# A planner's order of work gets a string of leanings, and a layernorm step is moved

## The chip, the cores and the metric

One core of a Trainium2 chip runs the kernel. The metric is the time of one execution in microseconds (us), the median of several runs. The engines are TensorE (PE, matrix products; PEld is its weight loading), VectorE (DVE), ScalarE (ACT), GpSimd (POOL) and SyncE (SP, which here issues transfers). Each engine works through its own instructions in program order; semaphores tie the engines together.

## What is computed

A block of attention with a gate, on x of 2048 tokens by 1024, in fp32:

```python
xn = _layernorm(x)
s  = softmax(q k^T / sqrt(32)) v @ wo          # 32 heads of 32, q, k, v = xn @ wqkv
h  = xn @ w1 + b1                               # 1024 -> 3584
act = h * tanh(softplus(h))                     # mish
return x + s * silu(act @ w2)                   # 3584 -> 1024
```

## The kernel before, in words

Every large product is made of three fast ones: an fp32 operand is split into a high part and the rest ("low"), and high x high, high x low and low x high are added in PSUM (`THREE`, line 281). The scores and P·V have their own forms: a head's 32 rows of high and low parts are stacked to a contraction of 128, and P·V is four narrow matmuls side by side.

**Opening, v stage (lines 447 to 527).** The 16 tiles of 128 tokens are normalised and transposed, and the first half of v is made from them. For tile t: `ln_a` (VectorE statistics), `ln_r` (ScalarE logarithm and exponential of the variance), `ln_b` (four small VectorE steps), `ln_x` (ScalarE scales the tile), `ln_t` (TensorE transposes it, eight times 128x128), `ln_c` (ScalarE copies the high part out of PSUM, VectorE the low part, for two halves). `v_group(i, t, cut, between)` issues the 24 products of one tile and calls `between`, here the next tile's transposes, after `cut` of them. The loop at line 474 runs these as a pipeline: the products of tile t - 2, the copies of tile t - 1, the scaling of tile t. Later in this stage the second half of v is made.

**qk stage (lines 664 to 683).** q and k of four heads at a time, with the first score products of head 0 and their maxima between them. `later` is a heap of small steps that are due some ticks ahead; `later.flush()` at line 682 issues what is left, the last small transposition of head 0's maxima ("mtp", `turn`) among it.

**Scheduled stage (lines 694 to 1240).** All heads of the attention and the whole feed-forward part run together, in an order that `Plan` works out while the program is built. An `Op` has an engine, an expected duration (`MM` = 0.228 us a matmul), the Ops it needs, buffers that it takes and gives back ("rings": seven PSUM banks `b`, of which s, t and d may hold 2, 2 and 4), and perhaps a `key`, the time at which it is due. `Plan.run` (line 173) simulates the engines: for the engine that is free first, it takes among the Ops that are ready the one with the least key, `(not op.late, key)` at line 194, emits it, and adds its duration. What comes out is a fixed order of instructions on each engine; on the chip each one waits for its real semaphores. TensorE's candidates come from five streams:

- t (line 812): scores, transposed, followed by ScalarE's exponentials "p"; then GpSimd adds up the sums "z" (line 841), and P·V ("pv", line 859) follows in groups of 6, 5 and 5 key tiles (`GROUPS`, line 35), with the column sums "zp" behind the last
- s (line 730): scores of the next head, of which VectorE takes the maxima "mx" (line 736)
- h (line 993): xn @ w1, 24 products for one tile of 128 features and 512 tokens, followed by the twelve steps of mish on VectorE and ScalarE
- y (line 1083): act @ w2, added up by VectorE into yacc (line 1105)
- op (line 1182): the first part of the product with wo, when the rest runs out

At line 703 the plan is told when each PSUM bank comes free of the stage before it; its five engines all start at 0.

**End (lines 1244 to 1312).** The rest of the product with wo, times silu, plus x.

Of the kernel before, what the change touches and what calls it, by code (L numbers as in the profile page):

```python
# [45 lines left out]


class Later:

# [20 lines left out]
class Op:  # L70


    def __init__(self, eng, took, need=(), emit=None, take=(), give=(), key=None, col=False, late=0.0,
                 bytes_=0, then=None, first=False, both=False, urgent=0.0):
# [3 lines left out]
        self.end = None  # L78


class Plan:
# [62 lines left out]
    def do(self, op, when):  # L144
# [71 lines left out]
def body(ctx: ExitStack, tc: tile.TileContext, x, wqkv, wo, w1, b1, w2, out):  # L216
# [504 lines left out]
    def s_stream():  # L721
        for h in range(1, H):
# [3 lines left out]
            for qt in range(NT):  # L726
                for kc in range(4):
# [5 lines left out]
                    def mx(at, h=h, qt=qt, kc=kc, tiles=tiles):  # L733
                        if qt == 0 and kc == 0:
# [3 lines left out]
                    m = Op("PE", MM, key=slot * (16 * (h - 1) + qt + (kc + 1) / 4 - LEAD), need=[loaded[h]],  # L738
                           emit=mm, take=["s", "b"])
                    yield m  # L740
# [57 lines left out]
    def t_stream():  # L798
        pts = {}
        for T in range(NS):  # L800
# [4 lines left out]
            for c in range(4):  # L805
# [14 lines left out]
                m = Op("PE", MM, key=slot * (T + (c + 1) / 4), emit=mm, take=["t", "b"],  # L820
                       need=[m_there[h, c]] if (h, c) in m_there else [])
# [29 lines left out]
    def product(T, pts, size):  # L851
# [15 lines left out]
        if kt == NT - 1:  # L867

            need.append(adds[T])
        last_pv[h] = op("PE", PV * size, key=slot * (T + 1.5), need=need + [vt_[h]], emit=emit, col=True,  # L870
                        take=["o"] if kt == size - 1 else [], give=["v"] if kt == NT - 1 else [], then=then)
# [107 lines left out]
    def h_stream():  # L979
        for n in range(NC * FT):  # L980
# [7 lines left out]
            for k in range(KT):  # L988
                for a, b in THREE:
                    def mm(at, n=n, c=c, k=k, a=a, b=b, i=i, t=t):  # L990
                        if i == 0:
# [4 lines left out]
                    give = (["w1"] if last else []) + ([f"xc{k // HK}"] if f == FT - 1 and (i + 1) % (3 * HK) == 0 else [])  # L996
                    m = Op("PE", MM, key=tile_time * due, emit=mm,
                           need=([w1_ops[n]] if n else []) + ([xc_ops[c, k // 2 * 2]] if c else []),
# [9 lines left out]
    def mish(n, made, t):  # L1008
# [42 lines left out]

        o1 = op("DVE", 0.74, need=[made], emit=d1, take=["e"])
        p1 = op("ACT", 0.73, need=[o1], emit=a1)
        p2 = op("ACT", 0.69, need=[p1], emit=a2, take=["d", "b"], first=True)
        o2 = op("DVE", 0.75, need=[p1], emit=d2)
        p3 = op("ACT", 0.68, need=[p2], emit=a3, take=["r"])
        o3 = op("DVE", 0.69, need=[o2, p2], emit=d3, give=["e"])
        p4 = op("ACT", 0.73, need=[p3], emit=a4)
        o4 = op("DVE", 0.69, need=[p4], emit=d4)
        o5 = op("DVE", 0.69, need=[o4], emit=d5, give=[("d", p2), ("b", p2)])  # L1060
        o6 = op("DVE", 0.69, need=[o5, o3], emit=d6, give=["r"])
        p5 = op("ACT", 0.6, need=[o6], emit=a5, take=["act"])
        act_ops[n] = op("DVE", 0.69, need=[p5], emit=d7, give=[("d", t["own"]), ("b", t["own"]), "h"])

# [3 lines left out]
    def y_stream():  # L1068
        for m in range(W2S):
            w2_op(m, [m_there[0, 3]])  # L1070
        for B in range(NC * FT // YB):
            c, b = divmod(B, FT // YB)
            done = []
            for dh in range(2):
                for s in range(4):
                    t = {}
                    for j in range(YB):
                        n, m_ = YB * B + j, (B * 2 + dh) * YB + j
                        for i, (p, q) in enumerate(THREE):
# [11 lines left out]
                            m = Op("PE", MM, key=tile_time * due, emit=mm,  # L1091
                                   need=[act_ops[n], w2_ops[m_]], take=["d", "b"] if j == 0 and i == 0 else [], give=give,
# [248 lines left out]
```

## Time and profile before

| what | before |
|---|---|
| median of 3 runs | 3411.41 us (3411.32 to 3413.32) |
| the profiled execution | 3414.67 us |
| its span, first to last instruction | 3412.9 us |
| TensorE busy | 3389.4 us (99%) |
| VectorE, ScalarE, GpSimd busy | 2337.6, 1955.3, 2431.8 us |
| TensorE's mean granted clock | 0.999 |

A row of the timeline gives start, length, engine, line, what is written from what, and how many instructions are merged in it; in brackets stands the engine's idle time before it and what ended that. A row of a group gives the count, the busy time, the mean of one in ns, the idle time ahead of the group's instructions and what ended most of it. A row of a window gives its length, the busy time of PE, PEld, DVE, ACT and POOL with their counts, the granted clock, the share of the DMA engines and GB/s. Matmuls are pipelined: their rows overlap.

### The profile page before, as it was taken

The page shows a single profiled execution, that of the slowest core. Times are in us where ns is not written, and L with a number is a line of the kernel's source. Part 1 is how long each engine was busy: PE and PEld are TensorE (multiplying, and loading weights), DVE is VectorE, ACT ScalarE, POOL GpSimd, SP SyncE. Part 2 cuts the span into 40 slices and gives each one's busy share as a digit, 9 for nine tenths or more (in the row PEclk, how much of TensorE's full clock was granted, in tenths as well). Part 3 has the DMA queues.
Part 4 walks back from the last instruction along what each step waited for, and adds up shares of the span by engine and source line. Part 5 has one row for each costly group of instructions (what it writes and reads, how often), then busy time and mean ns, then how long its engine had stood idle before and what let it go on. Part 6 is the DMA issues. An engine that isn't in the chain of part 4 may idle for free.

```text
span 3412.9 us, 45611 instructions
## 1 busy us (share of the span) xinstructions
PE 3389.4 (99%) x17059; PEld 2493.5 (73%) x17059; DVE 2337.6 (68%) x3764; ACT 1955.3 (57%) x3112; POOL 2431.8 (71%) x724
## 2 busy tenths in 40 slices
PE   8999999999999999999999999999999999999999
PEld 7888887677777777777777677777777677777687
DVE  6111136877878777787878777877878788876533
ACT  5211113766667667666666676666666666666621
POOL 1333333988899998888888888888888888888700
PEclk9999999999999999999999999999999999999999
DMA  5977877433444454343334543343445443333482
GB/s 196 297 268 269 277 266 249 121 112 100 123 130 129 139 173 145 103 124 106 118 102 122 156 142 115 109 126 98 129 114 181 125 118 112 112 118 119 136 298 84
DMA packets 284321, 517.02 MB, mean 151 GB/s; under 512 B 88170, under 2 KB 134250, under 8 KB 261354
## 3 DMA queue, kind: packets, MB, share of 16 engines
q1 hardware_dynamic: 264244, 472.16, 45.1%
q10 hardware_dynamic: 19856, 41.95, 3.3%
q8 instruction: 135, 2.21, 0.3%
q14 instruction: 86, 0.70, 0.1%
HBM read 374.31 MB, written 138.67 MB: 150 GB/s over the span
## 4 chain that ended last, share of the span: by engine, by line
PE 97%; DVE 1%; DMA 1%; ACT 1%; issue 0%; SPq 0%; POOL 0%; ACTq 0%; DVEq 0%
PE y L1083 18%; PE h L993 18%; PE t L812 13%; PE s L730 13%; PE pv L859 13%; PE qk L656 10%; PE op L1182 5%; PE v L337 5%; PE zp L885 1%; DVE mx L736 1%; PE pt L400 0%; ACT p L268 0%; PE s L583 0%; DMA xr<-xs 0%; DMA w2r<-in_B_w_dram 0%
## 5 line engine op out<-in xcount | busy, mean ns | idle before, releaser
L841 POOL TENSOR_TENSOR z<-z,p 128x2048 f32<-128x2048 f32 x448 | 2066.8, 4614 | 170.5 <-ACT p L268 142.0
L268 ACT ACTIVATE p<-t,zero 128x512 f32<-128x512 f32 x2048 | 1384.4, 690 | 622.6 <-PE t L812 608.0
L736 DVE TENSOR_REDUCE mx<-s 128x1 f32<-128x512 f32 x1984 | 1329.3, 686 | 440.9 <-PE s L730 433.7
L1083 PE MATMUL y<-w,act 128*128 128x512 f32 x2688 | 935.5, 391 | 0.7 <-DVE yacc L1105 0.5
L812 PE MATMUL t<-qstack,kstack 128*128 128x512 f32 x2048 | 802.2, 393 | 0.7 <-ACT p L268 0.5
L730 PE MATMUL s<-kstack,qstack 128*128 128x512 f32 x1984 | 778.8, 394 | 1.4 <-DVE mx L736 1.1
L993 PE MATMUL h<-xr,w 128*128 128x512 f32 x2016 | 713.6, 391 | 2.1 <-ACT p L268 1.2
L1083 PEld LDWEIGHTS y<-w,act 128*128 128x128 f32 x2688 | 502.7, 188 | 120.7 <-issue 9.2
L812 PEld LDWEIGHTS t<-qstack,kstack 128*128 128x128 f32 x2048 | 384.3, 188 | 111.8 <-issue 19.5
L859 PE MATMUL pv<-p,v 128*32 128x512 f32 x4096 | 459.4, 594 | 0.0
L730 PEld LDWEIGHTS s<-kstack,qstack 128*128 128x128 f32 x1984 | 371.2, 188 | 119.1 <-issue 21.0
L993 PEld LDWEIGHTS h<-xr,w 128*128 128x128 f32 x2016 | 377.8, 188 | 85.5 <-issue 5.0
L656 PE MATMUL qk<-xc,qkw 128*128 128x512 f32 x1536 | 350.8, 389 | 0.0
L656 PEld LDWEIGHTS qk<-xc,qkw 128*128 128x128 f32 x1536 | 288.2, 188 | 59.9
L859 PEld LDWEIGHTS pv<-p,v 128*32 128x32 f32 x4096 | 123.3, 110 | 282.8 <-issue 282.1
L1105 DVE TENSOR_TENSOR yacc<-yacc,y 128x512 f32<-128x512 f32 x416 | 283.0, 681 | 51.9 <-PE y L1083 51.0
L841 POOL TENSOR_TENSOR z<-p,p 128x2048 f32<-128x2048 f32 x32 | 148.0, 4626 | 219.7 <-ACT p L268 144.7
L993 PE MATMUL h<-xc,w 128*128 128x512 f32 x672 | 241.8, 392 | 0.1
L279 DVE TENSOR_TENSOR qst<-qk,qst 128x512 fp32r<-128x512 f32 x64 | 44.3, 692 | 257.6 <-ACT qst L271 257.6
L271 ACT ACTIVATE qst<-qk 128x512 fp32r<-128x512 f32 x64 | 38.3, 598 | 307.1 <-PE qk L656 291.7
L644 POOL CAST pw<-praw 128x512 fp32r<-128x512 f32 x64 | 39.5, 618 | 232.4 <-DMA w1s<-pw 123.7
L337 PE MATMUL v<-vw,xc 128*128 128x512 f32 x768 | 181.3, 395 | 1.8 <-ACT xc L271 1.3
(94 smaller groups left out, 2370.8 us busy)
## 6 DMA issues: line engine op xcount, KB each, us to landing
w<-w1s SPq DMA_DIRECT2D x112, 1024.0 KB
w<-w2s SPq DMA_DIRECT2D x200, 512.0 KB
qstack<-qs SPq DMA_DIRECT2D x96, 256.0 KB
kstack<-ks SPq DMA_DIRECT2D x96, 256.0 KB
x<-in_A_x_dram SPq DMA_DIRECT2D x32, 512.0 KB
praw<-in_B_w_dram SPq DMA_DIRECT2D x64, 256.0 KB
qs<-qst ACTq DMA_DIRECT2D x32, 512.0 KB
w1s<-pw SPq DMA_DIRECT2D x32, 512.0 KB
```

What stands on the lines that cost most here:

```text
L268: nc.scalar.activation(out_, in_, fn, bias=zero if bias is None else bias, scale=scale)
L337: nc.tensor.matmul(ps, xc[t // 4][k // HK][:, a, k % HK, (t % 4) * P:(t % 4 + 1) * P], vw[i, k // 2][:, b, k % 2], start=n == 0, stop=n == ...
L656: nc.tensor.matmul(ps, w[:, a, k], xc[c][k // HK][:, b, k % HK], start=n == 0, stop=n == 3 * KT - 1)
L730: nc.tensor.matmul(sp_, qst[h % 3][:, qt * P:(qt + 1) * P], kst[h % 3][:, kc * 512:(kc + 1) * 512], start=True, stop=True)
L736: nc.vector.reduce_max(tiles["mx"][:, qt, kc:kc + 1], tiles[qt, kc], axis=AX.X)
L812: nc.tensor.matmul(tp, kst[h % 3][:, kt * P:(kt + 1) * P], qst[h % 3][:, c * 512:(c + 1) * 512], start=True, stop=True)
L841: nc.gpsimd.tensor_tensor(zs[h], pts[T - 1] if kt == 1 else zs[h], pts[T], ALU.add)
L859: nc.tensor.matmul(pv[h][c * DH:(c + 1) * DH, :], vt[h][:, k, :], pts[T - kt + k][:, c * 512:(c + 1) * 512], start=k == 0, stop=k == NT - 1)
L993: nc.tensor.matmul(t["h"], w1t[n][:, a, k], xts_[c][k // HK][:, b, k % HK], start=i == 0, stop=i == 3 * KT - 1)
L1083: nc.tensor.matmul(t["y"], acts[n][:, p, s * P:(s + 1) * P], w2t[m_][:, q], start=j == 0 and i == 0, stop=j == YB - 1 and i == 2)
L1105: nc.vector.tensor_tensor(ya, ya, t["y"], ALU.add)
L1182: nc.tensor.matmul(ps[t, dh], ohl[t // 4, k][:, a, s * P:(s + 1) * P], wt[k][:, b, r], start=k == 0 and i == 0, stop=k == KT - 1 and i == 2)
```

## The change

The choice among ready Ops gets a leaning in each 21 us of TensorE's planned time, one of nine, read from a string of 130 digits. Digit 0 changes nothing. Digit 1 makes the key of the mish steps 2 us smaller (earlier); 2 and 3 let a P·V group count as ready 2 or 4 us later while TensorE is in the wide shape; 4 makes the key of s 6 us larger (later); 5 that of t 4 us larger; 6 those of h and y 8 us smaller; 8 that of h 8 us larger. Digit 7 ("settled") puts TensorE's Ops that became ready less than 0.2 us ago behind all others of their class. Further, the plan starts with VectorE busy until 2.8 us. And in the opening tile 2's `ln_a`, `ln_r` and `ln_b` stand behind `ln_c(1)`, and tile 1's `v_group` has its cut at 18 products instead of 8.

```diff
+LEANINGS = ({}, {"mish": 2.0}, {"hold": 2.0}, {"hold": 4.0}, {"s": -6.0}, {"t": -4.0}, {"h": 8.0, "y": 8.0}, {"settled": 1.0},
+            {"h": -8.0})
+TURN = 21.0
+LEAN = ("83700575777567776073778780867478770777713777737708777777777777788"
+        "87070875777277747776787770073777876777775777777787567766771872000")
...
+    def lean(self):
+        n = int(self.at["PE"] / TURN)
+        return LEANINGS[int(LEAN[n])] if n < len(LEAN) else {}
...
+            lean = self.lean()
...
+                    if op.kind == "pv" and not self.col:
+                        r += lean.get("hold", 0.0)
...
-                    key = (not op.late, r - op.urgent if op.key is None else op.key)
+                    key = (not op.late, e == "PE" and now - r < 0.2 and "settled" in lean,
+                           (r - op.urgent if op.key is None else op.key) - lean.get(op.kind, 0.0))
...
     v_low(0, 7, nc.vector)
-    ln_a(2)
-    ln_r(2)
     xts[3] = x_load(3)
     for t in range(2, NT + 2):
-        if t < NT:
+        if 2 < t < NT:
             ln_b(t)
-        evac = v_group(0, t - 2, 21 if t == 2 else 8, (lambda: ln_t(t - 1)) if t <= NT else None)
+        evac = v_group(0, t - 2, {2: 21, 3: 18}.get(t, 8), (lambda: ln_t(t - 1)) if t <= NT else None)
         if t <= NT:
             ln_c(t - 1)
+        if t == 2:
+            ln_a(2)
+            ln_r(2)
+            ln_b(2)
         if t < NT:
             ln_x(t)
...
     plan.rings["b"] = [(t, i) for i, t in enumerate((0.0, 0.2, 0.3, 0.9, 1.5, 2.1, 2.7))]
+    plan.at["DVE"] = 2.8
```

The other lines of the diff give the Ops their kind: "s", "t", "h", "y", "pv" and "mish".

More of the change, by code (lines that the diff above doesn't have):

```diff
@@ L73, in __init__ @@
     def __init__(self, eng, took, need=(), emit=None, take=(), give=(), key=None, col=False, late=0.0,
-                 bytes_=0, then=None, first=False, both=False, urgent=0.0):
+                 bytes_=0, then=None, first=False, both=False, urgent=0.0, kind=None):
         self.eng, self.took, self.need, self.emit = eng, took, need, emit
@@ L77, in __init__ @@
         self.bytes, self.then, self.first, self.both, self.urgent = bytes_, then, first, both, urgent
-        self.end = None
+        self.kind, self.end = kind, None
 class Plan:
@@ L738, in s_stream @@
                     m = Op("PE", MM, key=slot * (16 * (h - 1) + qt + (kc + 1) / 4 - LEAD), need=[loaded[h]],
-                           emit=mm, take=["s", "b"])
+                           emit=mm, take=["s", "b"], kind="s")
                     yield m
@@ L818, in ex @@
                     act(pts[T][:, c * 512:(c + 1) * 512], tile_[0], AF.Exp, scale=SCALE)
-                m = Op("PE", MM, key=slot * (T + (c + 1) / 4), emit=mm, take=["t", "b"],
+                m = Op("PE", MM, key=slot * (T + (c + 1) / 4), emit=mm, take=["t", "b"], kind="t",
                        need=[m_there[h, c]] if (h, c) in m_there else [])
@@ L869, in product @@
             need.append(adds[T])
-        last_pv[h] = op("PE", PV * size, key=slot * (T + 1.5), need=need + [vt_[h]], emit=emit, col=True,
+        last_pv[h] = op("PE", PV * size, key=slot * (T + 1.5), need=need + [vt_[h]], emit=emit, col=True, kind="pv",
                         take=["o"] if kt == size - 1 else [], give=["v"] if kt == NT - 1 else [], then=then)
@@ L996, in h_stream @@
                     give = (["w1"] if last else []) + ([f"xc{k // HK}"] if f == FT - 1 and (i + 1) % (3 * HK) == 0 else [])
-                    m = Op("PE", MM, key=tile_time * due, emit=mm,
+                    m = Op("PE", MM, key=tile_time * due, emit=mm, kind="h",
                            need=([w1_ops[n]] if n else []) + ([xc_ops[c, k // 2 * 2]] if c else []),
@@ L1050, in d7 @@
                                            op0=ALU.mult, op1=ALU.subtract)
[L1052 to L1063, printed above, removed]
+        o1 = op("DVE", 0.74, need=[made], emit=d1, take=["e"], kind="mish")
+        p1 = op("ACT", 0.73, need=[o1], emit=a1, kind="mish")
+        p2 = op("ACT", 0.69, need=[p1], emit=a2, take=["d", "b"], first=True, kind="mish")
+        o2 = op("DVE", 0.75, need=[p1], emit=d2, kind="mish")
+        p3 = op("ACT", 0.68, need=[p2], emit=a3, take=["r"], kind="mish")
+        o3 = op("DVE", 0.69, need=[o2, p2], emit=d3, give=["e"], kind="mish")
+        p4 = op("ACT", 0.73, need=[p3], emit=a4, kind="mish")
+        o4 = op("DVE", 0.69, need=[p4], emit=d4, kind="mish")
+        o5 = op("DVE", 0.69, need=[o4], emit=d5, give=[("d", p2), ("b", p2)], kind="mish")
+        o6 = op("DVE", 0.69, need=[o5, o3], emit=d6, give=["r"], kind="mish")
+        p5 = op("ACT", 0.6, need=[o6], emit=a5, take=["act"], kind="mish")
+        act_ops[n] = op("DVE", 0.69, need=[p5], emit=d7, give=[("d", t["own"]), ("b", t["own"]), "h"], kind="mish")
     w2_took, w2_uses, w2_ends = {}, {}, {}
@@ L1090, in y_stream @@
                             due = YB * B + YB + Y0 + g * Y1 + (BEHIND if B >= NC * FT // YB - 2 else 0)
-                            m = Op("PE", MM, key=tile_time * due, emit=mm,
+                            m = Op("PE", MM, key=tile_time * due, emit=mm, kind="y",
                                    need=[act_ops[n], w2_ops[m_]], take=["d", "b"] if j == 0 and i == 0 else [], give=give,
```

## The prediction

> **What bounds the kernel now.** I read the page first, for the busy shares; then the groups of TensorE's instructions, for their counts and for the idle time ahead of them; then the timeline, for what one of each costs when nothing holds it up; then the granted clock in short windows.
>
> ```profile
> span 3412.9 us, 45611 instructions
> ## 1 busy us (share of the span) xinstructions
> PE 3389.4 (99%) x17059; PEld 2493.5 (73%) x17059; DVE 2337.6 (68%) x3764; ACT 1955.3 (57%) x3112; POOL 2431.8 (71%) x724
> ```
>
> ```profile
> L1083 PE MATMUL y<-w,act 128*128 128x512 f32 x2688 | 935.5, 391 | 0.7 <-DVE yacc L1105 0.5 <-ACT p L268 0.2
> L812 PE MATMUL t<-qstack,kstack 128*128 128x512 f32 x2048 | 802.2, 393 | 0.7 <-ACT p L268 0.5
> L730 PE MATMUL s<-kstack,qstack 128*128 128x512 f32 x1984 | 778.8, 394 | 1.4 <-DVE mx L736 1.1
> L993 PE MATMUL h<-xr,w 128*128 128x512 f32 x2016 | 713.6, 391 | 2.1 <-ACT p L268 1.2 <-DMA xr<-xs 0.8
> L859 PE MATMUL pv<-p,v 128*32 128x512 f32 x4096 | 459.4, 594 | 0.0
> ```
>
> ```profile
> L885 PE MATMUL zp<-z,ones 128*32 128x512 f32 x256 | 33.3, 592 | 0.4 <-POOL z L841 0.4
> L400 PE MATMUL pt<-ident_r,x 128*128 128x128 f32 x128 | 18.4, 291 | 9.0 <-ACT x L268 9.0
> ```
>
> ```profile
> L560 PE MATMUL mtp<-ident_r,hl 128*128 128x128 f32 x35 | 8.8, 250 | 2.9 <-DVE hl L279 2.9
> ```
>
> TensorE is the bound: 99% busy against 71% for the next engine. But its rows overlap (a row lasts 0.39 us and the next may begin sooner), so "busy" also hides short waits. What it loses is found by counting from start to start.
>
> ```profile
> 560.60 5.60 PE L656 MATMUL qk<-xc,qkw 128*128 128x512 f32 x24
> 566.04 1.07 PE L583 MATMUL s<-kstack,qstack 128*128 128x512 f32 x4
> ```
>
> ```profile
> 923.99 0.39 PE L993 MATMUL h<-xc,w 128*128 128x512 f32 x1
> 924.31 5.36 PE L859 MATMUL pv<-p,v 128*32 128x512 f32 x48
> 929.60 0.50 PE L812 MATMUL t<-qstack,kstack 128*128 128x512 f32 x1
> 929.94 0.40 PE L730 MATMUL s<-kstack,qstack 128*128 128x512 f32 x1
> ```
>
> ```profile
> 3408.46 0.69 DVE L1275 TENSOR_TENSOR y<-op,y 128x512 f32<-128x512 f32 x1 [3.95 <-PE op L1182]
> ```
>
> A full matmul costs (566.04 - 560.60) / 24 = 0.2267 us. One of the narrow pv records costs (929.60 - 924.31) / 48 = 0.110 us. Going into the narrow shape costs 924.31 - 923.99 - 0.227 = 0.09 more, coming out 929.94 - 929.60 - 0.227 = 0.11.
>
> Now the floor. Of 17059 records 4096 + 256 are narrow, 128 are transposes and 35 the small mtp; 12544 are full: 12544 x 0.2267 = 2843.7. Narrow: 4352 x 0.110 = 479.6. The shape changes 3 times per head (GROUPS, line 35, has three entries; zp rides behind the last), 96 x 0.20 = 19. Transposes 128 x 0.1 and mtp 35 x 0.1: 16. Sum 3358. The span leaves 3412.9 less about 8.4 (nearly all of the 9.0 ahead of the transposes lies before the first) less 4.4 behind the last matmul (3412.9 - 3408.46) = 3400. So TensorE loses **about 42 us in all**, and no order of its work gains more. I split this into three places: the opening, 8.4 to 35.4 (72 products and 32 transposes, 19.5 of 27.0, so 7.5 lost); the seam ahead of the scheduled stage, 2.9 of waiting and 1.7 of half clock, 4.6; and the rest, some 29, spread over that stage.
>
> **The opening (v stage).** These rows are TensorE, ScalarE and VectorE around the second and third token tile.
>
> ```profile
> 17.45 1.09 PE L400 MATMUL pt<-ident_r,x 128*128 128x128 f32 x8 [0.66 <-ACT x L268]
> 18.30 0.95 PE L337 MATMUL v<-vw,xc 128*128 128x512 f32 x3
> 20.55 0.73 PE L337 MATMUL v<-vw,xc 128*128 128x512 f32 x2 [1.31 <-ACT xc L271]
> 21.50 2.35 PE L337 MATMUL v<-vw,xc 128*128 128x512 f32 x6 [0.22 <-DVE xc L279]
> 23.65 1.91 PE L400 MATMUL pt<-ident_r,x 128*128 128x128 f32 x8
> 25.21 5.93 PE L337 MATMUL v<-vw,xc 128*128 128x512 f32 x24
> 30.98 1.04 PE L400 MATMUL pt<-ident_r,x 128*128 128x128 f32 x8
> ```
>
> ```profile
> 19.39 0.29 ACT L268 ACTIVATE rs<-var,zero 128x1 f32<-128x1 f32 x1 [2.00 <-DVE var L370]
> 19.72 0.29 ACT L268 ACTIVATE rs<-rs,zero 128x1 f32<-128x1 f32 x1
> 19.92 1.06 ACT L271 ACTIVATE xc<-pt 128x512 fp32r<-128x512 f32 x2
> 20.88 1.25 ACT L268 ACTIVATE x<-x,tmp,rs 128x1024 f32<-128x1024 f32 x1
> ```
>
> ```profile
> 17.64 1.28 DVE L368 BATCH_NORM_STATS2 st<-x 128x6 f32<-128x512 f32 x2
> ```
>
> ```profile
> 31.61 1.09 ACT L271 ACTIVATE xc<-pt 128x512 fp32r<-128x512 f32 x2 [1.66 <-PE pt L400]
> ```
>
> ```profile
> 32.24 1.29 DVE L279 TENSOR_TENSOR xc<-pt,xc 128x512 fp32r<-128x512 f32 x2 [2.72 <-ACT xc L271]
> ```
>
> Tile 1 is transposed at 17.45, but ScalarE copies it only at 19.92: it stands behind tile 2's logarithm, which waits until 19.39 for VectorE's statistics begun at 17.64. The diff puts statistics, logarithm and scale of tile 2 (ln_a, ln_r, ln_b; no DMA, so no queue moves) behind ln_c(1). In the steady rows the copies start 31.61 - 30.98 = 0.63 after the transposes and VectorE's lows 0.63 after that. So copies at 18.1, lows 18.7 to 20.0, and TensorE's first product of tile 1 moves from 20.55 to about 19.0, when the three at 18.30 are out.
>
> Tile 2 pays for it. Statistics from 20.0; the logarithm 19.39 - 17.64 = 1.75 later, 21.8; logarithm and exponential 0.62; the scaling starts 20.88 - 20.01 = 0.87 after them, 23.3, and ends 1.25 later, 24.55. Before, the transposes of tile 2 began at 23.65; the new cut of 18 puts 18 products ahead of them, 19.0 + 18 x 0.227 + 0.4 for tile 1's lows = 23.5. TensorE idles 1.1, transposes 24.6 to 25.5, and does the last six products until 26.8. VectorE has then done statistics of tiles 3 and 4 (1.75 each) and one scale, so tile 2's first low ends near 28.1, against two products available: TensorE idles 0.85 more. From 28.1 come 22 products and 8 transposes: the third group ends near 34.1. Before: 16 of the 24 at 25.21 are the second group, 8 the third; the transposes end at 31.8; 16 x 0.227 more is 35.4. **Gain 1.3.** Later tiles are TensorE-bound, so it is kept. ScalarE's evacuation of group 0 slips by 1.5 us, with eight banks to cover it.
>
> One thing can take it back: the clock.
>
> ```profile
> 15.40:18.80 3.40, 2.74 (x15) 2.12 (x16) 3.26 (x9) 0.81 (x1) 0.00 (x0) 1.00 0.57 182
> 18.80:22.20 3.40, 1.88 (x7) 0.91 (x7) 2.54 (x10) 2.70 (x5) 0.00 (x0) 1.00 0.01 2
> 22.20:25.60 3.40, 3.40 (x14) 2.90 (x13) 3.23 (x10) 1.61 (x5) 0.00 (x0) 0.50 0.00 0
> 571.80:575.10 3.30, 3.30 (x10) 2.54 (x10) 1.84 (x3) 1.57 (x4) 0.00 (x0) 0.50 0.91 214
> ```
>
> First number after the length is TensorE's busy time, third from the end its clock. 1.88 busy of 3.40 is followed by half clock for 3.4 us; 2.74 is not. My two idles fall in different windows and leave about 2.4 and 2.6 busy, nearer to 2.74, so I count full clock. At half clock 1.7 us are lost and the opening ends 0.4 behind: its range is -0.4 to +1.7.
>
> The Trainium skill, "TensorE: Matmul & The Clock Gate", section "Why this matters for your kernels", asks only for "No PE-idle gaps >~3µs between matmul bursts". By that rule neither idle could cost clock and the gain would stay 1.3. The trace disagrees with it: the longest idle before the drop at 22.2 was 1.31 us.
>
> **The seam.**
>
> ```profile
> 570.07 0.33 PE L560 MATMUL mtp<-ident_r,hl 128*128 128x128 f32 x1 [2.91 <-DVE hl L279]
> 570.39 0.70 PE L730 MATMUL s<-kstack,qstack 128*128 128x512 f32 x2
> ```
>
> ```profile
> 567.47 2.48 DVE L587 TENSOR_REDUCE mx<-s 128x1 f32<-128x512 f32 x4
> ```
>
> TensorE stands 2.91 us, and 571.8 to 575.1 goes at half clock (1.7 more). One would expect `plan.at["DVE"] = 2.8` to cure that, for VectorE's four maxima end at 567.47 + 2.48 = 2.8 after TensorE comes free. It doesn't: this mtp comes from `later.flush()` (line 682), ahead of anything the plan places. The plan's zero is then really 570.39, when VectorE is free. The plan will hold back the third s product, and the small turn of head 0, by about 2.8 us; TensorE fills in with h, of which one tile is 24 x 0.227 = 5.4 us. Cost 0, hidden by that tile; if the next weights are late, 1 at most; gain at most 1. VectorE loses some 2 us here and has 32% of idle time to recover.
>
> **The scheduled stage.** `kind=` and `lean()` issue nothing; they reorder the same instructions, so the floor stays. 78 of the 130 digits are 7 (among TensorE's candidates, one that became ready under 0.2 us ago stands back), 13 are 0. The rest shift h and y by 8 us of due time, t by 4, s by 6, a product pv by 2 or 4, the mish by 2.
>
> What can be had? The idle named in the group rows: 0.7 + 0.7 + 1.4 + 2.1 + 0.4 = 5.3, from some ten waits. Each hides another 0.39 - 0.23 = 0.16, together 6.9. The other 22 of the 29 is 2 ns on each of some 10000 matmuls: waits too short for a row, and matmuls that are simply slower, which no order cures. A product just released is exactly where the plan's clock and the chip's differ, and TensorE's queue is in order, so one that is late holds up all the others: digit 7 removes waits up to 0.2 us and shortens longer ones by one matmul. Against that, each new order makes its own misses. I take the 6.9 and 0.3 of the short ones: **7.2** (an estimate; bounds: +13, twice the named ones, and -9, priced below).
>
> Sum: 1.3 + 0 + 7.2 = 8.5 off the profiled execution's 3414.67, its span of 3412.9 and 1.8 around it. That execution is 3.3 above the median of the timed runs, so I take the same 8.5 off 3411.41: **3402.9**.
>
> **The rivals.**
>
> A. The stalls only move. The named waits have four different causes (exponentials, maxima, a DMA, an addition), each a miss of the plan by 0.2 to 1.2 us, more than 7 covers. Then only the opening gains: 3410.1. For it: some stalls lie where two causes meet. Against: most are single waits behind s and t, which 7 is made for.
>
> B. The forecast, but the opening drops to half clock: 3404.6.
>
> C. Slower. Standing back means that each t product in a stretch of 7 can start one matmul later, 0.227, and t has two banks, so ScalarE's exponential starts later too. Over the stage ScalarE has 43% idle and it costs nothing; but where a mish shares it with the exponentials it is the local bound (the 1.2 us ahead of h is a wait for an exponential), and what it loses there TensorE loses. It takes (6.8 + 1.3) / 0.227 = 36 of the 2048 t products to be slower by 0.2%; with 2%, 41 of them, 9.3 us are lost: 3419.4.
>
> D. The order removes twice the named waits, 13: 3411.4 - 1.3 - 13 = 3397.1.
>
> **Numbers.** Forecast 0.55 (own range 3399 to 3407), A 0.17, B 0.10, C 0.10, D 0.08. Range 3395 to 3412: it leaves out C and a little of D's low end. A measurement tells about 0.2%, 6.8 us, from no change: faster means under 3404.6. Four fifths of the forecast, D and half of B: 0.56. Slower, C and little less: 0.09. Within: 0.35.
>
> **What would show it.** Tile 1's copies near 18.1, first product near 19.0, two idles near 1 us before 29, clock 1.0 throughout: the opening is right. The mtp still waits 2.9 near 570: the seam is right. Idle ahead of y, t, s and h under 2 us together instead of 4.9, at the same counts: the stage is right. Idle with new releasers of the same sum is A; longer idle behind exponentials is C. Wrong altogether if the seam's wait vanishes, or if narrow groups no longer stand as 96.

## The result, and the profile after

The changed kernel takes **3401.21 us** (median of 6 runs, 3400.82 to 3401.47). The kernel before, run beside it, takes 3413.2 (6 runs, 3411.32 to 3415.51). The ratio is 0.9964, interval 0.9953 to 0.9975, so the change makes the kernel faster by 12.0 us, or by 8.5 to 16 us with the interval. The profiled execution takes 3401.16 us, with a span of 3399.4, against 3414.67 and 3412.9.

The page of the changed kernel, with the lines that answer to the first fence of the prediction:

```profile
span 3399.4 us, 45612 instructions
## 1 busy us (share of the span) xinstructions
PE 3379.6 (99%) x17059; PEld 2498.3 (73%) x17059; DVE 2352.3 (69%) x3764; ACT 1960.5 (58%) x3112; POOL 2431.8 (72%) x724
```

The counts are the same (one instruction more in 45612), and TensorE is still 99% busy. The page shows that the kernel has become shorter, but not where. The groups of TensorE's instructions show a first part of it (count | busy, mean ns | idle time ahead and what ended it):

```profile
L1102 PE MATMUL y<-w,act 128*128 128x512 f32 x2688 | 932.6, 390 | 0.2
L831 PE MATMUL t<-qstack,kstack 128*128 128x512 f32 x2048 | 798.7, 392 | 2.3 <-DMA qstack<-mt 1.4 <-DVE mx L755 1.0
L749 PE MATMUL s<-kstack,qstack 128*128 128x512 f32 x1984 | 775.7, 393 | 0.0
L1012 PE MATMUL h<-xr,w 128*128 128x512 f32 x2016 | 704.4, 390 | 0.0
L878 PE MATMUL pv<-p,v 128*32 128x512 f32 x4096 | 459.3, 594 | 0.0
```

The idle time of y, t, s and h has gone from 4.9 us to 2.5, and 1.4 of these 2.5 are a new wait of t for a DMA, qstack<-mt, which does not stand in the rows of before. That is a gain of 2.4 us in a kernel that gained 13.5 in this execution, so the rest lies in times that these rows do not count.

I therefore counted from start to start, as the prediction did for its floor, but for every pair of TensorE's records: the distance of two starts, less what the pair costs when nothing holds it up (0.227 us between wide products, 0.318 from a wide one into the narrow shape, 0.523 from the last narrow one out of it, and 0.114 more for the next). What is left over is lost time. This table gives it in us for three places, and for the scheduled stage by the size of the single loss. One profiled execution of each kernel stands behind its row.

| kernel | opening, to 40 us | seam, 555 to 580 us | stage, 580 to 3240 us | of it losses to 12 ns | 12 to 150 ns | over 150 ns (how many) |
|---|---|---|---|---|---|---|
| before | 7.7 | 5.4 | 23.8 | 9.3 | 6.3 | 8.2 (17) |
| after | 6.0 | 8.7 | 9.3 | 3.8 | 3.8 | 1.7 (3) |
| difference | -1.7 | +3.3 | -14.5 | -5.5 | -2.5 | -6.5 |

The **stage** gained twice what I forecast, more than half of it in losses that no row of the profile names. The **opening** gained about what I said, and the **seam** lost 3.3, where I had said nothing.

The waits of TensorE in the stage (waited for: us in total, times, longest), before:

```profile
PE h L993 <- ACT p L268: 1.2, 1, 1.2
PE s L730 <- DVE mx L736: 1.1, 3, 0.5
PE h L993 <- DMA xr<-xs: 0.8, 1, 0.8
PE t L812 <- ACT p L268: 0.5, 1, 0.5
PE y L1083 <- DVE yacc L1105: 0.5, 1, 0.5
PE zp L885 <- POOL z L841: 0.4, 1, 0.4
PE y L1083 <- ACT p L268: 0.2, 1, 0.2
```

and after, where one line is all that is left:

```profile
PE t L831 <- DVE mx L755: 1.0, 1, 1.0
```

The timeline of TensorE at the seam of the changed kernel (start, length):

```profile
568.38 0.47 PE L578 MATMUL mtp<-ident_r,hl 128*128 128x128 f32 x1 [2.91 <-DVE hl L295]
568.69 1.19 PE L749 MATMUL s<-kstack,qstack 128*128 128x512 f32 x2
569.68 1.05 PE L831 MATMUL t<-qstack,kstack 128*128 128x512 f32 x2
570.54 0.63 PE L1012 MATMUL h<-xc,w 128*128 128x512 f32 x1
572.54 0.77 PE L831 MATMUL t<-qstack,kstack 128*128 128x512 f32 x1 [1.38 <-DMA qstack<-mt]
573.11 3.62 PE L1012 MATMUL h<-xc,w 128*128 128x512 f32 x8
```

The wait of 2.91 us is unchanged, as forecast. New is the third t product, placed behind a single h product: it waits 1.38 us for the stored maxima of head 0, while eight h products stand behind it in TensorE's queue. That h could have run is seen in the experiment e7 below, where three h products go there at 569.78. The rows show a second cost: two s products take 1.19 us instead of 0.70 before. The window over this place has half clock throughout (third number from the end):

```profile
567.60:577.70 10.10, 7.95 (x19) 5.88 (x20) 2.86 (x8) 2.58 (x6) 0.00 (x0) 0.50 0.83 258
```

In the kernel before, the half clock at the seam lasted 3.41 us; here the clock record runs from 567.51 to 577.75, 10.24 us, three times as long.

### The profile page after: what moved, and what is told of

Its sections match the earlier page's. It is cut to its first block, busy times and chain, and to the rows that moved or that the text cites. A ratio compares the mean times of both kernels' runs of the same rounds, so it can differ in the third digit from the quotient of the medians.

```text
span 3399.4 us, 45612 instructions
## 1 busy us (share of the span) xinstructions
PE 3379.6 (99%) x17059; PEld 2498.3 (73%) x17059; DVE 2352.3 (69%) x3764; ACT 1960.5 (58%) x3112; POOL 2431.8 (72%) x724
## 4 chain that ended last, share of the span: by engine, by line
PE 99%; DVE 1%; ACT 0%; DMA 0%; issue 0%; SPq 0%
PE y L1102 18%; PE h L1012 18%; PE t L831 14%; PE s L749 13%; PE pv L878 13%; PE qk L674 10%; PE op L1201 5%; PE v L353 5%; PE zp L904 1%; PE pt L416 0%; PE s L601 0%; DVE mx L755 0%; DVE st L384 0%; PE mtp L578 0%; DMA x<-in_A_x_dram 0%
## 5 line engine op out<-in xcount | busy, mean ns | idle before, releaser
L1012 PE MATMUL h<-xr,w 128*128 128x512 f32 x2016 | 704.4, 390 | 0.0
L1012 PE MATMUL h<-xc,w 128*128 128x512 f32 x672 | 232.2, 394 | 0.0
```

The source lines that it names most:

```text
L1012: nc.tensor.matmul(t["h"], w1t[n][:, a, k], xts_[c][k // HK][:, b, k % HK], start=i == 0, stop=i == 3 * KT - 1)
```

## The experiments

After reading the two traces I held two theories of the stage. One: the gain is that of digit 7. A product just released stands back, and so the many short misses between the plan's clock and the chip's disappear, whatever the order is otherwise. The rival: the gain belongs to the one order that this string of digits reaches, and any other order has misses of its own. For the opening the question was whether the move gains anything by itself, for the seam what had placed the third t product so early. The times of all experiments, each beside the kernel before (the ratio is that of the runs, with its interval):

| kernel | median us (runs) | ratio | opening | seam | stage | to 12 / 12 to 150 / over 150 ns (how many) |
|---|---|---|---|---|---|---|
| e1_opening_alone | 3412.41 (10) | 0.9995 [0.9985, 1.0004] | 6.0 | 5.5 | 23.7 | 9.1 / 6.0 / 8.6 (14) |
| e2_dve_alone | 3413.94 (10) | 1.0001 [0.9992, 1.001] | 6.1 | 5.6 | 23.9 | 8.9 / 6.4 / 8.7 (20) |
| e3_all_settled | 3411.49 (10) | 0.9993 [0.9983, 1.0002] | 6.1 | 5.2 | 22.6 | 2.2 / 8.0 / 12.4 (32) |
| e4_no_dve | 3398.85 (4) | 0.9956 [0.9941, 0.997] | 6.1 | 5.8 | 9.9 | 3.9 / 3.8 / 2.3 (4) |
| e5_no_settled | 3412.76 (10) | 0.9989 [0.9978, 1.0] | 6.1 | 7.8 | 21.0 | 8.2 / 6.3 / 6.4 (15) |
| e6_rotated | 3413.19 (10) | 0.9991 [0.9979, 1.0002] | 6.1 | 8.9 | 22.1 | 4.5 / 6.6 / 11.0 (23) |
| e7_first_digit | 3411.29 (10) | 0.9987 [0.9975, 0.9999] | 6.1 | 5.8 | 22.0 | 4.0 / 7.1 / 10.9 (27) |
| e8_early_turn | 3396.94 (4) | 0.9938 [0.9913, 0.9962] | 6.1 | 3.7 | 9.1 | 3.8 / 3.6 / 1.7 (4) |
| e9_early_turn_banks | 3399.57 (5) | 0.996 [0.9946, 0.9974] | 6.1 | 6.0 | 9.5 | 3.9 / 3.9 / 1.7 (3) |
| e10_middle_digit | 3401.28 (5) | 0.9965 [0.9952, 0.9978] | 6.1 | 7.7 | 9.4 | 3.8 / 3.8 / 1.8 (3) |
| e11_banks_no_dve | 3398.13 (4) | 0.9956 [0.9941, 0.9971] | 6.1 | 4.7 | 9.9 | 3.9 / 3.8 / 2.3 (4) |
| e12_maxima_by_act | 3394.18 (5) | 0.9947 [0.9933, 0.996] | 6.1 | 1.6 | 9.4 | 3.9 / 3.5 / 2.0 (3) |

The interval belongs to the ratio of all runs, which is not that of the two medians: for e8 the medians alone give 0.9950. The kernel before had medians of 3413.64 (beside e1 to e4), 3413.98 (e5 to e8), 3413.8 (e9 to e11) and 3412.97 (e12).

### e1: the opening alone

The kernel before, with the move and the cut of the opening and nothing else.

```diff
-    ln_a(2)
-    ln_r(2)
     xts[3] = x_load(3)
     for t in range(2, NT + 2):
-        if t < NT:
+        if 2 < t < NT:
             ln_b(t)
-        evac = v_group(0, t - 2, 21 if t == 2 else 8, (lambda: ln_t(t - 1)) if t <= NT else None)
+        evac = v_group(0, t - 2, {2: 21, 3: 18}.get(t, 8), (lambda: ln_t(t - 1)) if t <= NT else None)
...
+        if t == 2:
+            ln_a(2)
+            ln_r(2)
+            ln_b(2)
```

> The kernel before with the moved tile-2 steps and the cut of 18 alone; plan as before. Theory: the opening is worth what both traces show at the seam's small turn (570.07 before, 568.38 after), 1.7 us, and everything behind is shifted whole: 1.7 us faster than before, seam and stage losing what they lost before (about 5.4 and 24 us of TensorE time). Rival: the shift changes the phase of the clock's windows or of the transfers, and the rest moves by more than 1 us either way.

The median is 1.2 us below that of the kernel before, but the interval of the ratio holds 1: no gain that can be told from none. In the profile the opening loses 6.0 instead of 7.7. What that 1.7 is, e2 showed.

### e2: VectorE's start alone

The kernel before with `plan.at["DVE"] = 2.8` alone; its opening is the old one.

```diff
     plan.rings["b"] = [(t, i) for i, t in enumerate((0.0, 0.2, 0.3, 0.9, 1.5, 2.1, 2.7))]
+    plan.at["DVE"] = 2.8
```

> The kernel before with VectorE's planned start at 2.8 us alone. The forecast said 0, at most 1 us either way, since the wait at the seam comes from later.flush(). Rival: this line is what lets a t product in front at the seam whose maxima are still on their way, and makes the seam lose 3.3 us more, as in the changed kernel; then this is some 3 us slower than before.

The time is that of the kernel before, and stage and seam lose what they lost before. But this run settles the opening, by accident. Its timeline of TensorE there, with the old order:

```profile
20.51 0.73 PE L337 MATMUL v<-vw,xc 128*128 128x512 f32 x2 [1.31 <-ACT xc L271]
21.46 1.67 PE L337 MATMUL v<-vw,xc 128*128 128x512 f32 x6 [0.22 <-DVE xc L279]
22.96 1.03 PE L400 MATMUL pt<-ident_r,x 128*128 128x128 f32 x8
23.75 5.72 PE L337 MATMUL v<-vw,xc 128*128 128x512 f32 x24
29.31 1.03 PE L400 MATMUL pt<-ident_r,x 128*128 128x128 f32 x8
30.10 5.71 PE L337 MATMUL v<-vw,xc 128*128 128x512 f32 x24
```

From 17.4 to 21.5 everything stands as in the kernel before, to 0.04 us and with the same idle times to 0.01, but the six products then take 1.67 us instead of 2.35. The two windows that had shown the drop before show none here:

```profile
18.80:22.20 3.40, 1.88 (x7) 0.95 (x6) 2.54 (x10) 2.70 (x5) 0.00 (x0) 1.00 0.01 2
22.20:25.60 3.40, 3.40 (x20) 2.87 (x20) 3.19 (x10) 1.91 (x5) 0.00 (x0) 1.00 0.00 0
```

And this is the same place in the changed kernel, with the move:

```profile
17.44 1.10 PE L416 MATMUL pt<-ident_r,x 128*128 128x128 f32 x8 [0.16 <-ACT x L284]
18.29 5.16 PE L353 MATMUL v<-vw,xc 128*128 128x512 f32 x21
24.50 1.09 PE L416 MATMUL pt<-ident_r,x 128*128 128x128 f32 x8 [1.05 <-ACT x L284]
25.34 2.09 PE L353 MATMUL v<-vw,xc 128*128 128x512 f32 x8
27.78 1.66 PE L353 MATMUL v<-vw,xc 128*128 128x512 f32 x6 [0.34 <-DVE xc L295]
29.28 1.04 PE L416 MATMUL pt<-ident_r,x 128*128 128x128 f32 x8
30.07 5.71 PE L353 MATMUL v<-vw,xc 128*128 128x512 f32 x24
```

The last row is the same work in both: 30.10 against 30.07, and the first product of e2 had started 0.05 us earlier (8.31 against 8.36). At equal clock the move is worth under 0.1 us. It only divides one idle stretch into two smaller ones (1.31 + 0.22 becomes 1.05 + 0.34). The 1.7 us are the half clock, which in the old order comes in one execution and not in the other.

### e3: digit 7 everywhere

```diff
-LEAN = ("83700575777567776073778780867478770777713777737708777777777777788"
-        "87070875777277747776787770073777876777775777777787567766771872000")
+LEAN = ("77777777777777777777777777777777777777777777777777777777777777777"
+        "77777777777777777777777777777777777777777777777777777777777777777")
```

> The changed kernel with the digit 7 in all 130 places. Theory: standing back from what was just released is what removes the stage's waits, in any string; the stage then loses some 12 us against 9.3 in the changed kernel and 23.8 before, and the time is within 3 us of the changed kernel. Rival: the other 52 digits, fitted place by place, make the gain; then the stage loses 18 or more and the time is 8 us or more above the changed kernel.

The first theory falls. The losses up to 12 ns go from 9.3 to 2.2, further down than in the changed kernel, so standing back does what it says. But the losses over 150 ns rise from 8.2 to 12.4, and nothing remains. The waits of TensorE in the stage are others than before, with four exponentials ahead of t among them:

```profile
PE h L1012 <- DMA xr<-xs: 1.3, 1, 1.3
PE y L1102 <- DVE yacc L1124: 1.3, 3, 0.5
PE t L831 <- ACT p L284: 0.9, 4, 0.3
PE s L749 <- DVE mx L755: 0.6, 2, 0.4
PE t L831 <- DVE mx L755: 0.5, 1, 0.5
```

### e4: without VectorE's start

```diff
-    plan.at["DVE"] = 2.8
```

> The changed kernel without VectorE's planned start at 2.8 us. If that line makes the longer seam, the seam loses 5.4 again instead of 8.7 and the kernel is up to 3 us faster, unless the digits were fitted to the plan with it. If the first digit (8, h stands back) makes it, the seam stays at 8.7.

2.4 us faster by the medians than the change (the ratios' intervals overlap), and the seam accounts for it: 5.8 instead of 8.7. Without the line the plan gives the third s product earlier (569.95, ahead of h), the third t product goes at 572.53 after a wait of only 0.25 us, and the half clock there lasts 3.4 us. The stage keeps its gain, although TensorE's order starts out quite different; more on this under e10.

### e5: the other digits without the 7

Each 7 of the string becomes 0, the rest stays.

```diff
-LEAN = ("83700575777567776073778780867478770777713777737708777777777777788"
-        "87070875777277747776787770073777876777775777777787567766771872000")
+LEAN = ("83000505000560006003008080860408000000013000030008000000000000088"
+        "80000805000200040006080000003000806000005000000080560066001802000")
```

> The changed kernel with every 7 replaced by 0: the 52 other digits stay. Theory (standing back makes the gain): the stage loses 18 to 24 us as before, time 9 us or more above the changed kernel. Rival (the fitted digits make it): the stage loses 9 to 14, time within 5 us of the changed kernel.

The short losses are back at 8.2, the long ones stand at 6.4, and the time is within 1.2 us of the kernel before. So neither the 7 alone (e3) nor the rest alone gives the stage's 14.5 us.

### e6: the same digits at other places

```diff
-LEAN = ("83700575777567776073778780867478770777713777737708777777777777788"
-        "87070875777277747776787770073777876777775777777787567766771872000")
+LEAN = ("88707087577727774777678777007377787677777577777778756776677187200"
+        "08370057577756777607377878086747877077771377773770877777777777778")
```

> The changed kernel with the string rotated by 64 places: the same digits in the same numbers, at other places (it begins with 8 as before). Theory (standing back): the time stays within 4 us of the changed kernel. Rival (fitted to the places): the stage loses 18 or more, 8 us above it.

The same kinds of digits in the same number, put elsewhere: short losses 4.5, long ones 11.0, and no gain. The profiled execution behind this row took 3416.41, 3.2 above its median. Of its 11.0, 4.0 lie in a half clock from 656.99 to 663.81, behind a wait of 2.9 us for stored maxima; without it 7.0 are left, close to the 8.2 of the kernel before. The short losses thus follow the number of sevens; the waits do not.

### e7: one digit, at the start

The first digit, which holds for the first 21 us, becomes 7 instead of 8.

```diff
-LEAN = ("83700575777567776073778780867478770777713777737708777777777777788"
+LEAN = ("73700575777567776073778780867478770777713777737708777777777777788"
```

> The changed kernel with its first digit 7 instead of 8, so that h doesn't stand back in the first 21 us. Theory for the seam: 8 puts t's third product ahead of h while the maxima it needs are still being stored, and TensorE waits with h products at hand; with 7 the 1.4 us wait for that transfer goes and half clock lasts 3.4 us and not 10.2: the seam loses about 5.4 and not 8.7, up to 3 us faster. Rival: VectorE's planned start makes it, and the seam stays.

One digit of 130 takes the stage from 9.3 us lost back to 22.0, so that this kernel is 10 us slower than the change and not up to 3 faster, as I had expected. The seam is better for it, 5.8 instead of 8.7: digit 8 makes the key of h larger, so in the changed kernel h stands back in exactly the stretch in which only h can run, and with VectorE's line that put the third t product so early. It takes both: the seam loses 8.7, 7.8, 8.9 and 7.7 in the four kernels with the digit 8 and the line (the changed kernel, e5, e6, e10), 5.8 with the digit alone (e4), and 5.2 to 5.8 with the line alone (e2, e3, e7). The waits of the stage in this kernel:

```profile
PE t L831 <- ACT p L284: 2.4, 7, 0.6
PE s L749 <- DVE mx L755: 1.1, 2, 0.7
PE y L1102 <- DVE yacc L1124: 0.3, 1, 0.3
PE y L1102 <- ACT act L287: 0.3, 1, 0.3
PE t L831 <- DVE mx L755: 0.3, 1, 0.3
```

The largest is t behind exponentials, the row that rival C expected. It is 2.4 us and not 9.3. That the 7 makes it isn't shown: in e3, where every digit is 7, the same row has 0.9, and in the kernel before 0.5.

### e10: one digit, in the middle

The 65th digit, which acts from about 1910 us of the trace, becomes 7 instead of 8.

```diff
-LEAN = ("83700575777567776073778780867478770777713777737708777777777777788"
+LEAN = ("83700575777567776073778780867478770777713777737708777777777777787"
```

> The changed kernel with one digit of 130 altered, the 65th (8 to 7), which acts from about 1910 us. Theory (the string is fitted to one exact order, and an order once left isn't found again): up to 1910 the stage loses what the changed kernel loses there, behind it the waits over 150 ns come back, 3 to 6 us in all. Rival (each digit has its worth in its own 21 us): under 1 us lost, all near 1910 to 1931.

It is told here because it belongs to e7. After e3 to e7 my theory was that the string is fitted exactly: change one decision, and the order is never found again. This falls too. Time and losses are those of the changed kernel, and so is the order: I compared the two orders of TensorE's products place by place, and the share of places with the same product (the same one of its stream, counted from the start) in each 200 us from 600 to 3200 is 1.00, except for 0.67 in 1800 to 2000 us. In e4 it is 0.08 at 600 to 800 us, and then 0.83 to 1.00. In e7 it stays between 0.07 and 0.75, and in e3, e5 and e6 between 0.04 and 0.72. So the gain is there where the order is reached, and some disturbances heal while others do not. The seam has the same order as well and yet loses 7.7 and not 8.7, with a half clock of 6.83 us and not 10.24: that part of the seam's 3.3 belongs to the execution. Why e4 returns to it and e7 doesn't stays open.

### e8: the turn of the third maxima earlier

The 2.91 us of the seam come from `m_tail`: the maxima of head 0's third group are copied and turned seven to ten steps after they are ready, which is at the very end. Here they go at steps 2, 4 and 5.

```diff
-        for t, fn in ((1, r1), (7, r2), (9, r3), (10, r4)):
+        for t, fn in ((1, r1), (2, r2), (4, r3), (5, r4)):
```

> The changed kernel with head 0's small steps due earlier (ticks 2, 4, 5 and not 7, 9, 10), so that the turn of its third group isn't left to the flush behind VectorE's last maxima. If that turn is the cause of the 2.9 us wait and of the half clock behind it, the seam's 8.7 falls to 1 or 2: 6 to 8 us faster. Rival: TensorE waits as long at the plan's first product that needs VectorE, and little is gained.

3396.94, 4.3 us below the change by the medians, less than the 6 to 8 expected. The wait is gone, the profiled execution has no half clock at the seam, and another wait is uncovered. From 600 us on TensorE's order is that of the changed kernel place by place, and so it is in e9 and e12, so that these three differ from it at the seam alone. TensorE there:

```profile
565.64 0.39 PE L749 MATMUL s<-kstack,qstack 128*128 128x512 f32 x1
568.70 0.50 PE L749 MATMUL s<-kstack,qstack 128*128 128x512 f32 x1 [2.67 <-DVE mx L605]
```

The second s product takes a PSUM bank out of which VectorE still takes the last four maxima. The wait is nearly as long as the one removed. That it brings no half clock seems to be luck of this execution: a window of the clock ends at 567.66, in the middle of it. Of the four timed runs two have a mean clock of 1.000 (3396.20, 3396.24) and two of 0.999 (3397.64, 3399.26).

### e9: free banks first

As e8, and the plan is given the banks in the order in which they really come free.

```diff
-    for i in (7, 6, 3, 1, 4, 2, 0, 5):
+    for i in (2, 6, 3, 7, 4, 5, 0, 1):
```

> The kernel with the early turn, and the scheduled stage's PSUM banks renamed so that its second product gets a bank that is free at once, and not one that VectorE's last maxima still hold. Theory: the 2.7 us that TensorE still stands at the seam go, and the seam loses under 1.5 us against 3.7 with the early turn and 8.7 in the changed kernel: 2 to 3 us faster than the early turn alone, about 3394. Rival: it then waits for the next bank or for the first exponentials, and gains under 1.

The wait for the bank goes, and the kernel is not faster than e8 but slower by 2.6 us of the medians (the ratios' intervals overlap). TensorE runs on to 573 and then stands longer than ever:

```profile
573.09 0.39 PE L749 MATMUL s<-kstack,qstack 128*128 128x512 f32 x1
577.02 1.19 PE L831 MATMUL t<-qstack,kstack 128*128 128x512 f32 x2 [3.54 <-DMA qstack<-mt]
```

SyncE's queue in the same stretch shows why: the small store of head 0's last maxima is issued only at 572.31, behind a load of weights whose issue holds the queue for 4.14 us.

```profile
568.08 4.14 SPq L291 DMA_DIRECT2D w<-w1s  x1
572.31 1.32 SPq L291 DMA_DIRECT2D qstack<-mt  x2
```

### e11: e9 without VectorE's start

```diff
-    plan.at["DVE"] = 2.8
```

> As the kernel with early turn and renamed banks, without VectorE's planned start at 2.8 us. With the turn gone the plan's zero is the time at which VectorE still has 2.8 us to do, so the line is right here: without it the plan puts s products and the next turn ahead of VectorE's real time, and the seam loses 1 to 3 us more. Rival (as in the changed kernel, where leaving it out gained 2.3): the same or faster.

This expectation failed. With the turn gone I took the line to be right about VectorE, and to be missed. Without it the median is 1.4 us lower, and the seam loses 4.7 instead of 6.0. The line does no measured good in any of the three pairs (before and e2, e4 and after, e11 and e9).

### e12: the store from another queue

As e9, and the store of head 0's last maxima is issued by ScalarE instead of SyncE.

```diff
         def r6(at):
             for a in range(2):
                 move(qst[h % 3][96 + a:97 + a, first * P:(first + n) * P]
-                     .rearrange("o (t p) -> o t p", p=P), tiles["mt"][n * a:n * a + n, :])
+                     .rearrange("o (t p) -> o t p", p=P), tiles["mt"][n * a:n * a + n, :],
+                     None if h else nc.scalar)
```

> As the kernel with early turn and renamed banks; only head 0's last maxima are stored from ScalarE's queue and not from SyncE's, where in that kernel they were issued at 572.3 behind a weight transfer whose issue lasted 4.1 us, though ScalarE had them ready at 570.3. Theory (the seam's last wait is SyncE's order): the t product that stood 3.5 us goes at about 574 and not 577, the half clock behind it goes too, and the kernel is 2 to 4 us faster than that one (3399.6), about 3396.5. Rival (the 16 DMA engines are full with the weights, whoever issues): the landing stays near 577 and the time within 1 us of 3399.6.

**3394.18 us**, the lowest median of all: 18.8 us below the kernel before (ratio 0.9947, 0.9933 to 0.996). ScalarE issues the store as soon as it has copied the maxima:

```profile
570.44 1.80 ACTq L291 DMA_DIRECT2D qstack<-mt  x2
```

and TensorE has no wait at this place any more:

```profile
573.15 0.39 PE L749 MATMUL s<-kstack,qstack 128*128 128x512 f32 x1
573.41 0.70 PE L832 MATMUL t<-qstack,kstack 128*128 128x512 f32 x2
```

The seam loses 1.6 us and the clock is 1.00 from 560 to 580. From e9 to e12 that is 4.4 us of lost time less: the wait of 3.54 and the half clock that it brought both go. (By the medians it is 5.4 us, or 4.6 if each is taken against its own runs of the kernel before; the intervals of the ratios overlap.)

The earlier issue is only a part of it. The issue begins 1.9 us earlier (570.44 against 572.31), but the store's eight packets of 512 bytes end 3.3 us earlier: they run from 571.77 to 572.97 in e12, and from 575.96 to 576.23 in e9, where they start 2.3 us after their issue has ended and among the packets of the weights (8192 bytes each, from 572.85 on) that share their queue. In e12 such packets begin at 573.20, when the store has landed. Whether the other queue or the earlier time put the store ahead of them, no run takes apart. The Trainium skill, "DMA: Bandwidth & Descriptors", section "Issuing engines are not separate DMA queues", says that the DMAs of all issuing engines run on the same 16 DMA engines. Its table of rules adds that spreading them over the engines "only saves sequencer issue time". Such a saving is seen here, the 1.9 us behind one load's issue of 4.14; by the packets it doesn't cover the whole 3.3.

Whether e12 beats e8 isn't settled, since the intervals of their ratios overlap.

## Why the prediction was right, and where it wasn't

The forecast was 3402.9, the result 3401.21, inside the forecast's own range. But the sum came out by two errors of opposite sign, and the reason that I gave for the stage didn't hold, so that the closeness of the number is luck.

**The bound.** TensorE as the bound, the floor, and counting from start to start held. Before, the three places lose 36.9 us by the finer count, where I had about 42; 3.8 of the difference is the unhindered distance, 0.227 here and 0.2267 there, on 12544 products. The 96 changes of shape are still 96, and the narrow pv records have the same mean of 594 ns.

**The opening (1.3 forecast, 1.7 in the profile).** The schedule I wrote down is what the trace shows: tile 1's copies at 18.14 against 18.1, its first product right behind the three at 18.29, an idle of 1.05 against 1.1, and a second of 0.34 against 0.85. But the comparison was wrong. I measured my new schedule against an execution that held a half clock, and took "1.88 busy of 3.40 is followed by half clock" as a rule. In e2 the same stretch with the same 1.88 is followed by full clock. At equal clock the move gains under 0.1 us, and the 1.7 comes only where an execution of the old order happens to drop. The failed step is that one on the clock. One of the two traces of the old order drops there, and none of the twelve with the move, so the move may spare some executions the drop; how many isn't measured. The timed gain of e1 (1.2 us, its interval holds 1) can't be told from nothing.

**The seam (0 forecast, 3.3 lost).** That the mtp still waits 2.91 was right, and so was that VectorE's start doesn't cure it. The step that failed is "TensorE fills in with h". The first digit is 8, which makes h stand back just there, and together with VectorE's line, which holds back the third s product, it put first a t product that the chip could not yet do. Either alone leaves the seam at 5.2 to 5.8 (e2, e3, e4, e7). I had listed what each digit does, and had not applied the first one to the first stretch. The wait costs 1.78 us from start to start, and the longer half clock the rest, of which the execution decides 1 us (e10).

**The stage (7.2 forecast, 14.5 gained).** For the named waits 6.9 were forecast and 6.5 measured (losses over 150 ns, from 8.2 to 1.7), but not by the step that I gave. That step, "digit 7 removes waits up to 0.2 us and shortens longer ones by one matmul", failed for the long waits: with 7 in every place (e3) the losses over 150 ns rise to 12.4, and from e3 to e7 and in e10 they stay low only where the order comes back to that of the changed kernel (e4, e10). I also wrote that most waits are single ones behind s and t; in the rows four of nine are theirs, 1.6 of 4.7 us, and the most time, 2.0, is that of h. Mis-sized was the term of the short losses, of which I wrote "waits too short for a row, and matmuls that are simply slower, which no order cures" and took 0.3. They gave 5.5 up to 12 ns and 2.5 from there to 150 ns, 8.0 together. That an order can take the short losses down is shown by e3 (9.3 to 2.2) and by e5, where they return with the sevens gone. How it does so is only argued. In the kernel before, counting losses to 12 ns alone, the ten products behind a loss of over 150 ns lose about 3.5 ns more each than the others (4.4 against 1.0), and a product that was released well before its turn may leave no such trail. No run takes this apart, nor says why this one order has so few long waits.

**The rivals.** A, that stalls only move, is what e3, e5, e6 and e7 show: four orders out of the same planner, all within 2.7 us of the kernel before by their medians. Their stages lose 21.0 to 22.6 against 23.8, in other places. I gave it 0.17, which was too little for a change of order as such; that this order does better is a property of this order. B did not occur in the changed kernel. C's row appears in e7 at 2.4 us, a quarter of my price. D's 13 us from the order did come in size (14.5), but not as twice the named waits: 8.0 of them are losses to 150 ns. The seam took a part of them back.

## What to carry to other kernels

Where an engine is 99% busy, count its time from start to start against the unhindered distance and add the losses up by place and by size: here it found 23.8 us in the stage where the rows of idle time named 5.3, and it kept apart three places that the total had mixed. Before a gain is credited to a change of order, disturb the order (rotate it, change its first step): here an order was worth 14 us in the stage by where it ended up, while the rule alone (e3) and the other digits alone (e5) brought no gain that the times can tell. And when a wait goes, look at once for the next thing in line (here a bank, then a queue), for the third removal gave what the second had not.

## What the runs showed of the hardware

**The half clock comes in whole windows, and their phase decides.** Behind the opening its lengths are 3.41 us (before, twice), 6.83 (e10) and 10.24 (after), so one, two and three windows. The clock came up at 11.97 in the kernel before and at 13.45 in e2, though their first products start at 8.36 and 8.31, and the windows can be counted on from there. In the kernel before one ran from 18.80 to 22.21 and held all of the 1.53 us of idle time around tile 1's copies: half clock followed. In e2 the windows end at 20.28 and 23.69, and the same idle time lies in two of them: no drop.

TensorE's busy time doesn't tell which window brings the drop. The first of these two in e2 also holds idle time ahead of the transposes, and its 1.80 us busy are fewer than the 1.88 that were followed by half clock in the kernel before:

```profile
16.86:20.28 3.42, 1.80 (x11) 1.32 (x11) 2.63 (x8) 1.39 (x4) 0.00 (x0) 1.00 0.31 114
20.28:23.69 3.41, 2.97 (x15) 2.21 (x16) 3.27 (x10) 1.83 (x4) 0.00 (x0) 1.00 0.01 2
```

What does separate them in these traces is the unhindered time of the products that start in a window (0.227 us a wide one, 0.11 a narrow one or a transpose, 0.06 the small turn): 1.36 us in that window of the kernel before, 1.55 in this one of e2. In all fourteen traces, every window at full clock that half clock followed has at most 1.42, and every other at least 1.55. This is a count behind the fact, and no run was made to test it.

The Trainium skill, "TensorE: Matmul & The Clock Gate", Part 1, says that the window is 3413 ns long and "free-running", and that "it doesn't reset when your kernel starts". These runs agree, with lengths of 3.41 us and its multiples and with the two times at which the clock came up.

**A load's issue can hold a queue for 4.14 us.** The load of w1s that stands at the seam took 1.28 us to issue in the changed kernel and 4.14 in e9. I had counted what a DMA takes until it lands, and not what its issue keeps waiting. In e9 a store of 4 KB in two parts stood behind it, and TensorE behind the store.
